# One TensorE, eight heads of attention and two mixers: the whole order of work written anew

## The chip, the cores and the metric

The kernel runs on one core of a Trainium2 chip. The metric is the device time of one execution in microseconds. The kernel before takes 292.22 us, the median of three runs (292.13 to 292.43).

## The reference

A block-sparse attention (each query block sees its neighbours, the first and the last block and three drawn blocks) over 4 batches, 8 heads, 768 positions and 64 elements is followed by a residual mixer: one linear layer over the 768 tokens, then a two-layer perceptron over the 512 channels.

```python
scores = np.where(mask, scale * (q @ k.T), -1e9)
attn = softmax(scores)
x = heads_side_by_side(attn @ v)                  # 4 x 768 x 512
a1 = alpha1 * x + beta1
u = x + lam * einsum('ts,bsd->btd', w_tok, a1)
a2 = alpha2 * u + beta2
out = u + lam * (maximum(a2 @ w_ch1, 0) @ w_ch2)  # 512 -> 2048 -> 512
```

## The kernel before

Two heads of one batch make a pair; there are 16 pairs, four to a batch. All of the work after a short preamble is written out as one long string, `ORDER`, of 1,589 words. A loop at the end of the kernel reads it word by word; the letters of a word pick a small function, the number says on which piece it works, and what follows a colon is a PSUM bank (for TensorE) or an engine (`d` VectorE, `a` ScalarE). Each engine, and each engine's DMA queue, then does its own words strictly in this order (`pin_order`); between engines an instruction waits for the data, the buffer or the bank that it needs (`bank_order` keeps one dependency per bank of the eight).

The words that the change and the prediction speak of:

- **lq, lk, lv** (line 437): load the queries, keys or values of a pair, with a cast to 16 bits, into one of six buffers (`NLD`). They are issued from GpSimd's queue, as are **lt** (two of the six slices of the token weights), **lc** (the small vectors: lam, alpha1 and beta1 spread over all partitions as lc0, lc1, lc2; be2T as lc4 and a2T as lc5), **lw** (line 479, one of four slices of the first channel weights, `w1b`) and **lx** (line 485, one of four slices of the second, `w2b`). A load of a pair from the eighth on waits for a flag that VectorE sets (**F**). The buffer of lx is that of the token weights, free when the last W is done.
- **cq, ck, cv**: copy the loaded pair to where it is used (line 421 on VectorE, 419 on ScalarE). This frees the load buffer.
- **H** (line 355): six transposes of a head's queries and keys into a bank; **hq, hk** copy them out. From pair 5 on a transposing DMA of SyncE's queue does this instead (**tq, tk**, line 593).
- **q** (lines 624 and 634): 1,024 columns of scores into two banks, banks 2j and 2j+1 for `:j`. Pairs 0 to 4 have nine such words each, in which the mask is 24 extra rows of the matmul; in the other pairs (line 634, 99 words) two 64-row matmuls run in two halves of the array and the mask is applied by VectorE (**m**). A word covers columns in order: q0 begins with the first key tile, q3 works on key tiles 4 and 5, and from q5 on (second half of a pair's nine) the pair's second head is used.
- **e** (line 645): the exponential of a q on ScalarE. **p, r** (line 661): its matmuls with the values. **n, nt**: the normalization.
- **a, b** (and halves ah, bh), **k** (line 763, 18 matmuls), **x**: the token mixer. **W** (line 496) and **w** turn the token weights; **L, S, T** fold lam and sums into weights; **U, u, v** turn the mixer's result into `uT`, with transposes on TensorE (U with a bank, line 806) or by DMA. **B** puts be2T beside it.
- **f** (line 828, four matmuls, one for each slice of w1b) and **g** (lines 842 and 844, behind a copy of a bias column for the first 16): the first channel layer with its maximum. **h** (line 907) and **o**: the second one. **Y, V, y, d, D**: the last two batches' first layer, in a scheme with fewer products.
- **M, N, O**: build the mask rows, write them to memory (line 538), read them back spread over the partitions (line 545). N and O stand in SyncE's queue with tq, tk, U by DMA and the stores **s**.
- **z**: a matmul of zeros of 480 columns, without use for the result. The preamble has more of them.

Before the words the preamble loads the first pair's queries and keys by separate queues, builds the mask, turns the first head, and copies it out in pieces:

```python
nc.vector.tensor_copy(out=kx[0][0:D, 0:P], in_=flatA[D:P, 0:P])      # line 393
nc.scalar.copy(out=qx[0][0:D, HS:S], in_=flatB[0:D, HS:S])
nc.vector.tensor_copy(out=qx[0][0:D, 0:HS], in_=flatA[0:D, 0:HS])
nc.vector.tensor_copy(out=kx[0][0:D, P:HS], in_=flatA[D:P, P:HS])
nc.vector.tensor_copy(out=kx[0][0:D, HS:S], in_=flatB[D:P, HS:S])    # line 397
```

Of the kernel before, what the change touches and what calls it, by code (L numbers as in the profile page):

```python
# [66 lines left out]
g10:a T1 f28:5 g26:a f20:4 g31:a T2 g25:a f16:1 ck8:a f7:2 a4 g4:a f23:6 g17:a T3 O0 f13:3 g7:a tq7  # L67
g28:a f18:0 cq8:d cv5:d g13:a f22:5 cv7:d tq6 g16:d g6:a f21:2 g23:d g22:a f27:1 g18:a tk8 P3:d
g20:a g21:d f14:3 g27:a P2:d f29:2 tk7 g14:a F34 b4 lk11 f30:0 g29:d lk9 tq8 cq11:d q53:2 g30:a
q48:1 P4:d k9:1 e53 lk12 A8 A0 lv8 e48 q50:3 q46:2 x9 h0:0 lq10 e46 A9 A1 h14:1 e50 A4 q52:1 o0  # L70
q49:2 e52 q45:3 A2 h1 A10 e49 h2 o12 A11 e45 h15 m48 P0:a F27 m50 lq9 q51:1 q47:2 m49 p48:6 e47 k8:7
F43 m45 m46 e51 p49 p50 o1 q58:2 x8 q56:1 e58 nt16 h16 m51 e56 m52 q60:2 q59:3 h3 o13 e60 A3 p45:2
m58 e59 p46 h17 m53 u8:a m47 u9:a q57:2 q55:3 F36 o2 e57 p47 U4 o14 p51:3 m59 h4 ck11:a m56 p52 e55
p53 nt15 lk14 q63:2 nt17 h18 e63 o3 q64:1 m57 q54:3 e64 q71:2 m60 h5 o15 e54 p57:2 a5 p58 h6 e71 b5
p59 ck12:a m64 q70:2 q62:3 nt19 e70 h19 lk10 m71 e62 q69:1 m54 q61:2 h20 F47 A5 ck9:a m55 p54:6
cq9:a k11:7 lv11 o16 e61 o4 tq9 lq13 h7:1 x11 cq10:a m62 k10:0 tk9 e69 m61 lv9 p60:7 A6 q67:2 tq10
m69 p55 e67 p56 o6 q80:1 x10 p61 e80 p62 nt18 q66:2 h8 nt20 e66 m70 q78:1 ck10:a q68:3 a6 p69:0 e68
p70 lk13 h9 m66 b6 e78 p71 o7 q65:2 q76:3 m63 u10:a q75:1 e65 nt23 h10 m67 u11:a p63:0 cv8:d k12:4
e76 m65 U5 lq12 m68 p66:5 e75 p64 x12 p67 tk10 p68 o8 q81:3 nt22 q86:1 e81 p65 h11 nt21 e86 m75
q74:2 q73:3 a7 e74 k13:0 b7 e73 q72:1 x13 q77:2 o9 u12:a k14:0 u13:a m76 e72 U6 k15:6 x14 A7 e77  # L80
p75:0 p76 x15 q79:1 u14:a m72 q85:2 u15:a h12 m77 e79 U7 m73 p77 e85 q82:3 m80 q93:1 s5 h13 m78 e93
tq11 m79 p78:4 p72:5 m74 e82 p73 p79 tk11 o10 p80 p74 q84:1 P1:d q87:3 nt24 e84 s0 f37:1 m86 tk12
f35:5 e87 nt26 f39:2 ck13:d g35:a m84 lq14 f54:3 g37:a nt25 g39:a q89:2 cv9:d q95:3 e89 q94:0 g54:d
lv10 f38:2 m82 e95 f32:3 P5:d P7:d f34:4 g32:a P6:d f48:5 e94 ck14:d m85 lk15 p84:3 a8 g34:a q83:3
q98:0 e83 p85 cq12:d f47:4 F44 F41 cv11:d tq12 lv15 m81 e98 p86 f61:6 g47:d lv12 g48:a p81:7 m83
q92:0 g61:a q88:2 b8 g38:a p82 f49:6 nt28 e92 m98 f36:2 e88 g49:d f63:3 m89 g36:a q106:0 m87 q91:2
g63:a p83 f51:6 e106 nt27 f56:2 m88 g51:a p87:3 cq13:d e91 f41:7 V0 m94 p88 g56:a q90:0 q96:2 cv10:d
g41:a m93 f52:2 e90 m92 p89 f57:6 m95 g52:a f53:7 e96 V2 p93:2 nt29 g57:a q97:0 q99:2 cq14:d e97
f33:3 m96 tq14 m91 p94 e99 p95 k16:6 m97 tk13 g33:a nt31 g53:a q104:0 m90 q102:1 s2 e104 q103:2 x16
f62:7 s1 a9 e102 tq13 p90:6 p91 p96:0 m99 p92 g62:a p97 nt30 tk14 p98 e103 f60:1 nt32 q113:1 m104  # L90
g60:a q100:2 s3 q105:3 e113 m102 s4 f59:0 b9 k17:1 e100 m113 F45 m103 lq15 e105 f55:2 x17 f44:3 lv14
g59:a m100 g55:a q108:2 m106 q107:0 lv13 e108 q101:3 m105 k18:2 a10 e107 p102:4 f50:5 m108 e101 x18
p99:0 p100 b10 g50:a f58:1 m101 g44:a p103 g58:a q131:3 m107 q115:1 p105:5 A20 e115 f45:1 A12 p106
e131 p104 A16 p101 p107 nt33 g45:a q112:1 k21:6 nt34 e112 nt35 q116:0 A21 q111:1 e116 q130:2 a11
# [5 lines left out]
p129:6 u19:a p130 m128 p131 e117 U9 k23:7 a12 e132 h40 o26 U10 nt43 cv15:a h41 x23 b12 u23:a q138:1  # L100
m127 q118:2 q119:3 e118 o34 h32 V5 cv13:a h21:0 m132 e119 m134 k25:4 o27 e138 k24:5 A14 x25 q142:1
o18 q143:3 A15 p126:4 p127 e143 x24 h33 m118 e142 p132:5 m117 h34 m138 p133 o28 p134 q141:1 nt44
q139:3 e141 p117:1 m143 p128 p118 h22 e139 nt42 m119 q135:1 a14 q125:2 e135 k22:6 b14 u24:a p119
# [975 lines left out]
```

## Time and profile before

| | |
|---|---|
| median of the runs, lowest, highest | 292.22, 292.13, 292.43 us |
| the profiled execution | 291.82 us |
| its span, first to last instruction | 290.1 us |
| granted TensorE clock | 1.0 throughout |
| busy: TensorE matmuls, weight loads | 283.9 us (98%), 213.6 us (74%) |
| busy: VectorE, ScalarE, GpSimd | 263.8 us (91%), 234.0 us (81%), 53.3 us (18%) |
| read from HBM, written | 31.16 MB, 6.88 MB |

The busy time of TensorE is modelled to the end of each matmul and so contains short waits. The chain of waits goes back from the last instruction to what released it, step by step; its pieces in order of time carry the start, the length, the engine and the line. For a load the view by tile gives the issue time and the time to landing. In the rows of stretches of time each engine's busy time stands with its count of instructions, then the clock, the DMA share (the sum over the packets in flight, so over 1 is possible) and GB/s.

### The profile page before, as it was taken

Reading aid. Unit: us, or ns where it says so; the run is one execution under the profiler, and the core shown is the slowest. Engines: PE = TensorE matmul, PEld = TensorE weight load, DVE = VectorE, ACT = ScalarE, POOL = GpSimd, SP = SyncE. Lnnn points to the kernel's source line nnn. Section 1 sums busy time; section 2 is a strip of 40 time slices with the busy share of each in tenths; the row PEclk is TensorE's granted clock in tenths of the full one; section 3 lists DMA queues with packets and bytes.
Section 4 is the critical chain, followed back from the end, with each engine's and each line's share of the span. In section 5 each row is a group of like instructions: output and inputs, shape, how many; then the busy total and the mean of one; then the engine's idle time right before and its main releaser. Section 6 shows DMA issues by size and latency. Waiting matters only on the chain.

```text
span 290.1 us, 8529 instructions
## 1 busy us (share of the span) xinstructions
PE 283.9 (98%) x3538; PEld 213.6 (74%) x3538; DVE 263.8 (91%) x595; ACT 234.0 (81%) x350; POOL 53.3 (18%) x102
## 2 busy tenths in 40 slices
PE   8899999999999999999999999999999999999995
PEld 3677888755677878866677877888766788866884
DVE  5689997689999999999999999999999998699983
ACT  5999998849999999999999999968989860279500
POOL 8545734300621241024005000000000000000000
PEclk9999999999999999999999999999999999999999
DMA  6999999999983498499278002404110140330014
GB/s 161 189 246 210 195 211 194 203 165 176 168 115 30 53 140 118 74 164 135 27 186 146 7 2 57 85 3 47 37 75 0 19 112 0 148 145 1 2 42 177
DMA packets 47927, 30.95 MB, mean 107 GB/s; under 512 B 28792, under 2 KB 43984, under 8 KB 47888
## 3 DMA queue, kind: packets, MB, share of 16 engines
q0 software_dynamic: 15936, 15.21, 34.6%
q1 hardware_dynamic: 31340, 14.32, 24.3%
q10 hardware_dynamic: 612, 0.87, 0.8%
q8 instruction: 28, 0.46, 0.6%
q14 instruction: 11, 0.09, 0.1%
HBM read 31.16 MB, written 6.88 MB: 131 GB/s over the span
## 4 chain that ended last, share of the span: by engine, by line
PE 87%; ACT 5%; DMA 4%; DVE 2%; issue 1%; POOL 0%; ACTq 0%
PE psum L907 26%; PE psum L997 13%; PE psum L828 12%; PE psum L661 11%; PE psum L763 11%; PE psum L634 9%; PE psum L624 4%; DMA wtk<-in_moe_w_tok_dram 3%; ACT hts L842 2%; ACT eT L645 2%; DMA k2f<-in_k_dram 1%; PE psum L806 1%; PE psum L355 1%; DVE a1p L733 0%; ACT rel L419 0%
## 5 line engine op out<-in xcount | busy, mean ns | idle before, releaser
L645 ACT ACTIVATE eT<-psum 128x1024 f16<-128x1024 f32 (+1 forms) x145 | 140.4, 1028 | 9.3 <-PE psum L634 5.4
L655 DVE TENSOR_TENSOR eT<-eT,maskT 128x960 f16<-128x960 f16 x99 | 61.2, 650 | 0.0
L907 PEld LDWEIGHTS <-hts 128*128 128x128 bf16 x480 | 45.1, 98 | 8.5 <-issue 2.1
L661 PEld LDWEIGHTS <-eT 128*128 128x128 f16 x1152 | 44.4, 97 | 8.3 <-issue 1.7
L661 PE MATMUL psum<-vext,eT 128*128 128x65 f16 x1152 | 48.5, 193 | 0.0
L828 PE MATMUL psum<-uT,w1b 128*128 128x384 bf16 (+1 forms) x256 | 45.9, 327 | 0.1
L1023 ACT ACTIVATE snap<-psum,b1t 128x384 f32<-128x384 f32 x44 | 23.7, 581 | 17.7 <-PE psum L997 13.4
L763 PE MATMUL psum<-a1p,wtokT 128*128 128x128 bf16 x576 | 36.8, 219 | 0.2 <-DVE x_sb L772 0.2
L763 PEld LDWEIGHTS <-wtokT 128*128 128x128 bf16 x576 | 33.2, 98 | 4.1 <-DVE x_sb L772 0.8
L907 PE MATMUL psum<-w2t,hts 128*128 128x256 bf16 x288 | 35.8, 273 | 0.0
L866 DVE TENSOR_TENSOR x_sb<-x_sb,psum 128x256 f32<-128x256 f32 (+1 forms) x61 | 30.7, 514 | 4.7 <-PE psum L907 4.5
L828 PEld LDWEIGHTS <-w1b 128*128 128x128 bf16 x256 | 23.0, 98 | 16.1 <-ACT b1t L419 0.9
L842 ACT ACTIVATE hts<-psum,b1t 128x384 bf16<-128x384 f32 x53 | 29.2, 602 | 0.9 <-PE psum L828 0.5
L634 PE MATMUL psum<-qx,kx 64*128 64x256 bf16 x396 | 29.8, 272 | 0.0
L866 DVE TENSOR_TENSOR hts<-snap,psum 128x384 bf16<-128x384 f32 x48 | 24.7, 547 | 2.7 <-PE psum L997 2.3
L624 PE MATMUL psum<-qx,kx 88*128 88x512 bf16 (+1 forms) x120 | 25.8, 326 | 1.3 <-ACT eT L645 1.0
L907 PE MATMUL psum<-w2b,ss 128*128 128x256 bf16 x192 | 24.6, 273 | 0.0
L907 PE MATMUL psum<-w2b,hts 128*128 128x256 bf16 x192 | 24.4, 273 | 0.0
L634 PEld LDWEIGHTS <-kx 64*128 64x128 bf16 x396 | 15.2, 94 | 8.4 <-issue 3.5
L907 PEld LDWEIGHTS <-ss 128*128 128x128 bf16 x192 | 18.0, 98 | 3.8 <-issue 0.6
L772 DVE TENSOR_TENSOR x_sb<-x_sb,psum 128x384 f32<-128x384 f32 x32 | 17.4, 546 | 1.0 <-PE psum L763 0.8
L997 PEld LDWEIGHTS <-w1b 128*128 128x128 bf16 x128 | 12.1, 98 | 6.6 <-DVE hts L866 0.3
(103 smaller groups left out, 362.5 us busy)
## 6 DMA issues: line engine op xcount, KB each, us to landing
out_dram<-x_sb SPq DMA_DIRECT2D x17, 256.0 KB, 2.6
v<-in_v_dram POOLq DMA_DIRECT2D x16, 192.0 KB, 6.3
k<-in_k_dram POOLq DMA_DIRECT2D x15, 192.0 KB, 6.2
q<-in_q_dram POOLq DMA_DIRECT2D x15, 192.0 KB, 7.1
w2b<-in_moe_w_ch_dram POOLq DMA_DIRECT2D x4, 512.0 KB, 12.0
w1b<-in_moe_w_ch_dram POOLq DMA_DIRECT2D x4, 512.0 KB, 12.9
wtk<-in_moe_w_tok_dram POOLq DMA_DIRECT2D x3, 384.0 KB, 8.3
out_dram<-x_sb SPq DMA_DIRECT2D x2, 512.0 KB
```

The lines of the kernel that those rows point to most:

```text
L624: nc.tensor.matmul(t[:, f : f + w], kx[h][0:KC, ts(jt, P)], qx[h][0:KC, c : c + w], start=True, stop=True,)
L634: nc.tensor.matmul(t[:, (2 * a + j) * TH : (2 * a + j + 1) * TH], kx[h][r, ts(2 * g + j, P)], qx[h][r, ts(th, TH)], start=True, stop=True,)
L645: nc.scalar.activation(eTs[n][:, c], t[:, c], AF.Exp, bias=EXPB, scale=SCALE)
L655: nc.vector.tensor_tensor(out=e, in0=e, in1=mask, op=ALU.min)
L661: nc.tensor.matmul(ops[key][:, t * VW : t * VW + D + 1], eTs[n][:, c : c + P], vext[n // NU % NV][:, a, jt, 0 : D + 1], start=(first and z ...
L763: nc.tensor.matmul(t[:, j, :], wtokT[:, s, ts(3 * g + j, P)], a1p[p][:, s, :], start=(s == 0), stop=(s == NT - 1),)
L828: nc.tensor.matmul(hps[i][:, 0:w], w1b[:, dk, ts(f, P)], uT[b][:, dk, hf * HS : hf * HS + w], start=(dk == 0), stop=(dk == 3),)
L842: nc.scalar.activation(hts[kk][:, f, :], t[:, 0:HS], AF.Relu, bias=b1t[:, f : f + 1], scale=1.0)
L866: nc.vector.tensor_tensor(out=out, in0=in0, in1=in1, op=op)
L907: nc.tensor.matmul(cps[b, q][:, side * HD : (side + 1) * HD], lhs[:, nk, :], rhs[:, nk, :], start=(z in (0, 6) and nk == 0), stop=(nk == H ...
L997: nc.tensor.matmul(chains[key], lhs[:, dk, ts(f, P)], rhs[:, dk, :], start=(z in (0, 1, 5) and dk == 0), stop=(dk == 1), skip_group_check= ...
L1023: nc.scalar.activation(dst, t, act, bias=bias, scale=1.0)
```

## The change

Nothing but the string `ORDER` is changed: the same 1,589 words (by kind and number) in another order, with other banks and in places another engine behind the colon. The order of GpSimd's loads is different: it began lv0 lk1 lq1 lt1 lq2 lk2 lv1 lq3 lt0 lt2 lk3 lc2 lc0 lc1 and begins lv0 lq1 lk1 lq2 lt1 lk2 lv1 lt0 lt2 lc1 lc2 lc0 lk3 lv2 lq3; the small broadcast vectors now stand ahead of the keys and queries of pair 3, the fourth pair of heads. The diff, cut after the first lines of each side (through the first f and g words):

```diff
 ORDER = """
-lv0 lk1 lq1 q0:0 lt1 q3:1 cq0 e0 lq2 q2:2 H1:6 lk2 e2 hq1:d q1:0 lv1 z480:7 hm0 z480:7 e1 hk1:d
-cv0:d q5:2 ck1:d e3 lq3 q4:0 p0:6 lt0 e4 p1 p2 lt2 q6:1 cq1:d e5 p3 lk3 p4 H2:7 H3:0 lc2 e6 hk2:d
-q7:2 lc0 F35 W2:1 hq2:d e7 lc1 q8:1 hq3:d r4:7 lk4 r5 w2:d e8 q9:2 cq2:d r6 F24 ck2:d lv2 r7 e9 n0
-z480:1 q12:1 lq6 hk3:d r8 e12 q11:2 n1 W3:6 q10:0 e11 w3:d H5:7 cv1:d q16:1 hk5:d e10 lq4 H4:6 hk4:d
-W1:4 e16 q15:0 hq5:d p9:5 e15 p10 hq4:d q13:1 F21 cq3:d W0:7 F46 w1:d e13 lv4 q14:0 p11 W5:4 e14
-ck3:d q25:1 F22 w0:d lk5 p12 w5:d e25 p13 q19:3 n2 W4:4 e19 H6:0 F28 lx3 w4:d q22:1 hk6:d r13:1
-q17:2 e22 L1 q20:3 hq6:d e17 q24:1 L0 r14 H7:0 e20 q18:2 ck4:d a0 lv3 r15 e18 r16 r17 lc5 b0 q23:3
-e24 cv2:d k1:4 n3 lk6 e23 lx1 q21:1 cq4:d r22:1 F42 x1 H9:5 e21 lv6 q28:3 F38 a1 p18:4 lw0 e28 r23
-F40 q26:1 b1 p19 e26 hk9:d p20 r24 p21 hq7:d r25 cq6:a q27:3 cv4:d hq9:d r26 lq7 e27 p22 q30:1 hk7:d
-k0:5 lw3 n5 e30 lc4 L2 H8:0 F23 F32 x0 q35:3 lw1 hk8:a hq8:d q31:1 lw2 k3:5 n4 e35 lx2 cv3:d q29:0
-ck5:a x3 lq5 q32:3 ck6:d e31 k2:4 lk7 a2 e29 lx0 b2 p27:5 q34:1 x2 lv7 p28 u0:d e34 p29 p30 u3:d p31
-lq8 r31:4 q33:0 e32 F37 n6 k4:2 e33 q39:3 x4 r32 u2:a F29 r33 e39 r34 r35 q37:0 n7 q38:1 U1:5 F25
-ah6 e38 q40:3 ah7 k5:4 cv6:d e37 bh7 lk8 bh6 q36:1 cq7:d e40 x5 k7:0 lv5 F33 u4:d e36 B0 k6:1 x7
-u1:a M0 p36:0 v1:a F39 u5:d p37 p38 x6 q41:1 u6:d U0:1 e41 q43:2 u7:d U2:6 S6 p39 e43 U3:7 v0:d
-q44:1 v2:a v3:d p40 q42:2 F26 S7 r40:1 r41 e44 f0:6 f6:7 e42 f3:2 g0:a f5:3 cq5:d g3:d f1:6 tq5 lq11
-g5:a F31 n8 r42 f8:2 N0 r43 g8:d f17:0 tk5 f24:3 r44 g24:d f9:2 tk6 S1 f11:3 g9:a g1:d f15:4 ck7:a
-S4 f25:2 g11:a n9 f19:5 F30 S3 f12:1 S2 f2:3 g12:a S0 f31:6 g19:a S5 g15:a f26:1 T0 g2:a f10:4 f4:3
...
+lv0 lq1 lk1 lq2 lt1 q3:0 q2:1 lk2 cq0 e3 q0:2 hm0 lv1 H1:6 e0 z480:7 hq1:d q1:0 lt0 z480:7 F41 F21
+hk1:d lt2 z480:7 e2 cv0:d lc1 q8:2 e1 q5:3 lc2 p0:2 lc0 e5 q4:0 lk3 p1 ck1:d e4 cq1:d q6:3 lv2 p2
+cq2:d H2:3 e6 lq3 F24 H3:0 hk2:d r4:1 p3 lq4 e8 p4 hq2:d q7:3 lw3 r5 n0 r6 e7 q10:2 lc5 hq3:d q9:1
+e10 lw1 ck2:d r7 hk3:d H4:6 lv3 r8 e9 hq4:d q13:2 W3:0 hk4:d e13 q11:1 w3:d q15:3 n1 e11 W2:0 H5:4
+w2:d W1:5 e15 q14:1 cv1:d hq5:d lk4 q12:0 e14 w1:d W0:6 W5:7 hk5:d W4:5 e12 F28 w0:d q16:1 p9:4
+w5:d e16 p10 q17:0 w4:d q23:3 L0 e17 q25:1 L1 r13:5 p11 e25 p12 ck3:d q22:0 a0 lv5 p13 e23 r14 r15
+lx0 n2 r16 r17 e22 q24:1 F37 b0 lc4 q18:3 F23 cv2:d e24 k0:4 n3 lq8 e18 q20:0 x0 r22:5 q19:1 cq3:d
+e20 a1 q26:3 lv4 H6:4 e26 r23 lw2 hk6:d q21:0 r24 b1 e19 r25 r26 hq6:d p18:6 H7:7 e21 n5 q28:1 p19
+F40 hq7:d e28 q30:2 F26 hk7:d p20 p21 e30 p22 cq4:d q27:0 F42 n4 lq5 q31:1 e27 k3:7 cv3:d lx2 F22
+e31 lx3 q32:0 x3 q33:2 e32 L2 lw0 q29:1 a2 lq7 p27:6 p28 e33 q35:0 b2 k2:7 ck4:d e29 F38 u0:d lv6
+H8:4 e35 B0 H9:5 x2 p29 hq9:d p30 hk8:a p31 r31:7 q34:0 hq8:d k5:2 u2:a hk9:d e34 n6 r32 q40:2
+cv5:a x5 k1:6 u5:d e40 lq6 F30 ah6 r33 q39:0 u3:a cv4:d F27 x1 lk7 r34 e39 r35 M0 q43:1 cq5:d
+q36:2 bh6 u1:a lv7 tq5 n7 q38:0 e43 k4:6 lx1 F29 ah7 N0 e36 bh7 q41:1 F46 x4 k7:7 e38 u4:d F47 S5
+e41 k6:6 S4 q42:0 F39 x6 U2:2 e42 x7 q37:2 cq8:d p36:3 u6:d r40:6 lk5 e37 U1:7 u7:d U0:0 r41 v0:d
+v2:a U3:1 p37 v3:d p38 v1:a r42 q44:2 S6 p39 e44 f1:2 r43 g1:a p40 f7:7 cv6:a r44 f11:2 n9 lk6
+f17:0 ck7:a n8 f18:1 cq6:a a4 f13:3 cv7:a F25 cq7:d f2:6 lk8 S7 g7:a f3:4 g11:d lq9 g13:a f27:5
+lk9 f12:7 g27:a f9:2 S2 f10:3 g17:d f15:5 g3:d f23:0 F32 F34 F36 g9:d f4:4 g23:a S3 f19:2 g2:a S0
+f29:0 g18:a g15:d f25:6 g10:a S1 f8:1 g19:a T0 g12:a f5:5 g4:a f14:7 ck5:d g25:a T1 tk5 f26:4 g8:a
+f0:6 g5:a T2 ck8:a f21:1 f16:5 g21:a ck6:d T3 tk6 f31:2 g0:a f28:1 g31:a b4 O0 f6:6 g14:a g26:d
...
 """
```

More of the change, by code (lines that the diff above doesn't have):

```diff
@@ L67 @@
[L67 to L94, printed above, removed]
@@ L100 @@
[L100 to L103, printed above, removed]
-e125 x22 h23 m141 u22:a q120:1 nt39 q140:2 e120 q137:3 U11 m142 k29:1 o19 e140 V1 k28:2 m125 u25:a
-x29 e137 p141:3 U12 p142 m120 p143 h24 u29:a m139 m140 q123:2 q121:3 o20 e123 p138:1 x28 p139 h25
@@ new lines @@
+q62:1 q71:3 m68 e62 p56 lq13 h18 nt18 e71 m61 q65:1 k10:0 o4 e65 m67 q69:3 cq12:a F35 o15 q66:1
+k11:4 e69 m63 s5 lv11 o6 tq10 h19 e66 x11 m65 q64:3 cq11:a tk10 q70:1 x10 p60:4 m62 u8:a p61 lk13
+h8 e70 m69 tq11 m66 p62 e64 h20 A6 U4 cv9:a nt20 q78:1 q73:3 m70 p66:0 u10:a lk12 h9 e73 o16 m64
+p63:4 p67 e78 p69:5 o7 p68 m71 q72:3 u11:a q75:1 a6 e72 p70 U5 h10 m78 e75 p64 b6 p65 q79:3 nt22
+cq13:a q80:1 p71 nt21 e80 k12:0 lq14 nt23 e79 o8 q86:1 x12 q84:2 h11 a7 e86 A7 q85:3 e84 q76:1 b7
+k13:0 e85 m79 k15:4 m80 P0:a x13 k14:5 o9 u12:a x15 e76 p78:0 x14 p79 q74:3 u13:a m72 h12 e74 m73
@@ new lines @@
+k16:0 tq12 cv10:a m95 e90 f33:1 nt27 lv12 cq14:d q94:2 x16 g33:a q92:3 q96:1 m90 e92 f34:0 tq14 a9
+f57:1 e94 f62:6 tk13 g57:d g34:a f50:7 m94 e96 p93:0 m92 s1 f39:1 g62:a tq13 m97 p94 g50:a p95 b9
+g39:a q107:1 m96 q103:2 s2 e107 q102:3 nt31 k19:1 m106 e103 p90:0 x19 p91 e102 p96:2 cv11:d p92
+ck14:d p97 nt30 p98 tk14 u16:a q113:2 nt32 q99:3 e113 f59:3 a10 q101:0 g59:a q100:2 m107 f58:2
+e101 m113 f37:3 e100 b10 f63:0 m101 e99 k18:1 F44 V4 lv14 m100 g58:a lv13 q105:2 g37:a m99 q116:3
+f56:2 g63:a V0 lv15 p99:3 m102 g56:a k20:0 e105 x18 m103 f32:2 e116 A20 p102:1 p103 p100 x20 g32:a
@@ new lines @@
+y123 D116:a y148:2 nt45 D130:a y142 d122:a p120:7 m123 p121 d147:a y132 d125 y154:6 d141:a d151
+y149 D123:a y141:0 D125:d V7 d148:a y161:1 y143 d144 y145:2 d142:a p122 d132 y150 d154:a d145
+p123:0 y144 d161:a a15 y156 d149:a y155:3 p124 d143:a nt40 y163 d155:a y151 d158 p125 D132:a b15
+y162:5 d162:a y146 nt41 y166:3 D138:a y152:7 d146 D139:a y164 a13 d150:a y157 y159:0 D144:a k30:2
+d152 d156:a b13 d163:a d165 y153 D151:a k26:4 d166 D146:a D158:a d153 D165:a y167 d159 k27:5
+D137:a x26 D153:d u26:a D166:d y160 D145:a x27 h42:7 d160 u27:a d167 D117:a h56:4 U13 D159:a
```

76 lines of the change are left out of this document (46 added, 30 removed).

## The prediction

> **What bounds the kernel now.** I read the page, then the chain of waits, then the instructions in order of time for the first microseconds, then single loads by tile.
>
> ```profile
> by line: PE psum L907 25.6%; PE psum L997 12.6%; PE psum L828 12.3%; PE psum L661 11.5%; PE psum L763 11.1%; PE psum L634 8.8%; PE psum L624 4.2%; DMA wtk<-in_moe_w_tok_dram 2.8%; ACT hts L842 2.0%; ACT eT L645 1.8%; DMA k2f<-in_k_dram 0.9%
> ```
>
> Seven lines of TensorE alone carry 86% of the chain. Its pieces (start, length, what) give the price of each kind of TensorE's work and the places where something else led.
>
> ```profile
> 5.83 1.61 PE psum L624 x9
> ...
> 10.70 8.27 DMA wtk<-in_moe_w_tok_dram
> ...
> 21.99 0.92 ACT eT L645
> ...
> 26.80 0.34 PE psum L355 x6
> 27.13 0.44 PE psum L624 x3
> 27.57 0.73 PE psum L661 x24
> 28.30 0.44 PE psum L624 x3
> 28.74 1.16 PE psum L763 x18
> ...
> 53.94 3.27 PE psum L828 x20
> ...
> 84.48 1.00 PE psum L763 x18
> ```
>
> The prices: a score word (q) of the first five pairs 0.44; one value matmul (p, r) 0.73/24 = 0.030; six transposes (H, W, U) 0.34; a token-mixing word (k) 1.00; a hidden-layer word (f, four matmuls) 3.27/5 = 0.65. An exponential of 1,024 columns holds ScalarE for 0.92.
>
> From 5.83, where the first score starts, to 53.94, where the hidden layer starts, lie 48.1 us. The words ahead of the first f (f0 in the order before) hold 45 q (19.8), 336 value matmuls (10.1), 8 k (8.0), 19 groups of six transposes (6.5) and three fillers of about 0.2 (0.6, 480 columns against 512 in the 0.22 piece that I take from the 0.44 of a q): 45.0. So TensorE waited about 3.1 us there. By 28.74 the same count (25 q, 144 value matmuls, 13 groups, the fillers: 20.4) leaves 28.74 - 5.83 - 20.4 = 2.5 of them. This is nearly all that another order can win, because the matmuls themselves are the same in both orders. One of the early waits is a load's: the chain stands on the token weights until 10.70 + 8.27 = 18.97, when W1 may start.
>
> **The change part by part.** The 1,589 words are the same; their order, the banks and some engines change. On ScalarE stand cv 9 times instead of 4, ck 3 instead of 8, cq 7 instead of 3, D 31 instead of 28, d 57 instead of 60, g and u one fewer each: two more in sum, at most 2 x 0.72 (a cast, below). I cost this at nothing, since TensorE's work hides it; if ScalarE led there it would be 1.4. Four of the casts get a price of their own below, for where they stand.
>
> *The start.* The first score is now q3 instead of q0. In order of time, from the kernel before:
>
> ```profile
> 6.39 0.11 PEld L624 LDWEIGHTS <-kx 88*128 88x128 bf16 x2 [0.18 <-DVE kx L397]
> ```
>
> q3 reads key tiles 4 and 5, which the copy of line 397 writes last; its weights waited for that copy until 6.39 there too, behind q0. So TensorE starts 0.56 later, and the first exponential comes at 6.39 + 0.44 + 0.1 = 6.95.
>
> *The first scores.* From there ScalarE sets the pace through the banks: a q may start when the exponential that emptied its bank has ended. The tightest such place in the new order, by counting, is q35, which follows the exponential e32: 32 exponentials end at 6.95 + 32 x 0.92 + 0.1 = 36.5. The TensorE work ahead of q35 (34 q, 232 value matmuls, 2 k, 13 groups, fillers) is 28.9, so 5.83 + 28.9 = 34.7, and 1.8 us of waits are forced, the late start included. The old order had 2.5 by 28.74. W1 is not held up any more: q3's load of pair 3 (lq3) now stands behind lt0 and lt2, so lt0 lands a head's load (1.0, below) earlier, at about 18.0, and W1 is due at about 18.9. Between 28.74 and 53.94 the old order gained another 0.6 of waits; with that TensorE would be ready for its first f (f1) at 5.83 + 45.1 (340 value matmuls) + 1.8 to 2.4 = 52.7 to 53.3, that is 0.6 to 1.2 before 53.94.
>
> *The loads ahead of f1.* Every f reads all four slices of w1b (lw0 to lw3). Loads by tile, with issue time and time to landing:
>
> ```profile
> L479 POOL DMA_DIRECT2D w1b<-in_moe_w_ch_dram x2: 571/576/581, 36.0 to 36.5; - x2
> DMA to landing us min/median/max: 14.3/14.9/15.6
> L485 POOL DMA_DIRECT2D w2b<-in_moe_w_ch_dram x1: 755/755/755, 38.5 to 38.5; - x1
> DMA to landing us min/median/max: 16.1/16.1/16.1
> L437 POOL DMA_DIRECT2D q<-in_q_dram x1: 706/706/706, 39.7 to 39.7; - x1
> DMA to landing us min/median/max: 15.9/15.9/15.9
> L485 POOL DMA_DIRECT2D w2b<-in_moe_w_ch_dram x1: 765/765/765, 44.4 to 44.4; - x1
> DMA to landing us min/median/max: 14.8/14.8/14.8
> L437 POOL DMA_DIRECT2D q<-in_q_dram x1: 713/713/713, 56.3 to 56.3; - x1
> DMA to landing us min/median/max: 11.1/11.1/11.1
> ```
>
> The last w1b slice (lw2) landed at 36.5 + 15.6 = 52.1, 1.8 before it was needed; lx2 at 54.6; lq5 at 55.6; lx0 at 59.2; lq11 at 67.4. Issue to landing is 11 to 16 us: the loads stand in one queue that never empties, so landings are a sum. A head's load costs 55.6 - 54.6 = 1.0; lk7 and lx0 together 3.6, so an lx 2.6. In the new order the last slice is lw0. Ahead of it and with it stand 16 head loads, all three lt, five lc, four lw and three lx; in the old order lx2 has the same with 18 head loads. So lw0 lands at 54.6 - 2 x 1.0 = 52.6, if nothing else uses the DMA engines.
>
> Something does. tq5 and N0, the first transposing DMA and the write of the mask rows, are issued right behind the cast of pair 5's queries (cq5) in both orders:
>
> ```profile
> 56.10 1.32 SPq L593 DMA_TRANSPOSE qx<-rel  x1
> 57.47 0.83 SPq L538 DMA_DIRECT2D mask_rows<-maskT  x1
> ```
>
> ```profile
> 45.00:56.00 11.00, 11.00 (x158) 8.59 (x156) 8.88 (x26) 10.18 (x13) 3.68 (x9) 1.00 1.18 203
> 56.00:60.00 4.00, 4.00 (x46) 2.68 (x44) 2.42 (x9) 0.81 (x3) 0.71 (x1) 1.00 1.40 188
> 60.00:64.00 4.00, 4.00 (x26) 2.18 (x24) 3.93 (x10) 2.21 (x6) 0.00 (x0) 1.00 1.39 119
> ```
>
> The last column is GB/s: 203 with the loads alone, then 188 and 119 when the others had joined. After lq5 the old kernel still got lk7 and lx0 in 3.6, without loss, and the next five head loads (to lq11) in 8.2 instead of 5.0: 3.2 lost. There that cost nothing, since f0 had started. In the new order lq5 stands ahead of lx2, lx3 and lw0, so tq5 and N0 go out at about 45 (52.6 less three large loads) and compete with them. lw0 comes 7.8 of load time after lq5; by the rows the loss is between 0 and (7.8 - 3.6)/5.0 x 3.2 = 2.7. It is nearer to the late rows, but there tk5 and tk6 were in the queue too, which now stand behind most of the f words; I take half, 1.3. Then lw0 lands at 53.9 and f1 starts at 54.0: **+0.1**, between -1.2 and +1.5.
>
> *Casts in ScalarE's queue.* Behind g1 the new order has cv6, ck7, cq6 and cv7 on ScalarE, and g7 behind them. Pieces of the chain of before:
>
> ```profile
> 66.92 2.00 ACT hts L842 x4
> 68.91 0.72 ACT rel L419
> ```
>
> A cast is 0.72, a g of this stage 0.50 and, with its small copy, about 0.65 (an estimate). With lw0's landing as zero, f1 starts at 0.1 and g1 ends at 1.5. The loads behind lw0 are lq7, lv6, lq6, lk7, lv7, landing at 1, 2, 3, 4, 5: cv6 ends at 2.7, ck7 waits for 4.0 and ends at 4.7, cq6 5.4, cv7 6.2, g7 6.8. f12 needs g7's bank and is reached after nine f and 20 value matmuls, 6.5 behind f1's start: 6.6. A wait of 0.2. With heads at 8.2/5 = 1.64 each it is 3.0 (lk7 6.6, lv7 8.2, g7 9.6). I take 0.5, nearer the first, since the tk transfers are not there.
>
> *Switches of the array.* From the sixth pair on the scores (line 634) use half of the rows each.
>
> ```profile
> 93.00 0.32 PE psum L634 x4
> 93.32 0.98 PE psum L907 x8
> 94.30 0.76 PE psum L634 x12
> 95.06 0.98 PE psum L907 x8
> 96.04 0.49 PE psum L661 x16
> 96.53 0.87 PE psum L907 x8
> ```
>
> An h word is 0.87, but 0.98 behind a run of such scores: 0.11. Eight more score matmuls make 0.32 into 0.76, so four are 0.22 and the other 0.10 of the 0.32 is the switch into the run. A run costs 0.2 beside its work. The old order groups the 99 score words in 46 runs, the new one in 49: 3 x 0.2 = **+0.6**. It lies on TensorE, which has no gap to hide it in; bounds 0 and 0.6.
>
> *What stays.* The work ahead of the first score and the last dozen words are the same. Pair 3's later keys and queries cost nothing: behind lt0 (18.0) lq3 has lt2 (twice a head's bytes, by its shape: 2.0), three small broadcast loads (at most 1.3 each, 4/3 of a head's bytes) and lk3, lv2 ahead of it, so it lands by 18.0 + 2.0 + 4.0 + 3.0 = 27.0. H6, which needs it, has 21.1 of TensorE work ahead: 5.83 + 21.1 + 1.8 = 28.7. If that cover of 1.7 were gone, each us more would be one lost.
>
> The sum: 0.1 + 0.5 + 0.6 = +1.2, on the profiled execution's 291.82, whose span is 1.7 less (both are in the table above), gives 293.0. The median of the runs shown is 292.22, 0.4 over that execution, and so the forecast is **293.4 us**.
>
> **The rivals.**
>
> (a) *The loads keep up.* No loss to tq5 and N0: lw0 at 52.6, f1 at about 53.0 (-0.9), f12's wait 0.2, switches +0.6: -0.1, 292.1. For it: 3.6 of load after lq5 went without loss. Against: 119 GB/s in the row that follows.
>
> (b) *Faster.* As (a), but early waits stay at 1.8, f1 starts at 52.7 (-1.2), and ScalarE, being half empty after the casts, no longer leads in the hidden layer, as it does in the chain before from 66.92 to 68.91 + 0.72 (I put 0.4 on such places, an estimate: half a g's length at two of them). -1.2 + 0.6 - 0.4 = -1.0: 291.2. It decides by lw0: landing before 52.7 it is possible, later not.
>
> (c) *The queues share evenly.* The loss is the full 2.7 (f1 at 55.4, +1.5), f12's wait about 1.5, switches 0.6: +3.6, 295.8. For it: by their shapes N0 writes three heads' loads of bytes and tq5 moves one, four against the 7.8 of load time that they meet. [...] The trace agrees from 60 on (119 GB/s, late heads) and not from 56 to 60.
>
> **How the numbers follow.** The forecast has 0.42, (a) 0.22, (b) 0.20, (c) 0.16. What the measurement tells from no change is 0.2%, 0.6 us: faster means under 291.6, slower over 292.8. (b) and an edge of (a) are faster: 0.24. (a)'s rest and a little of the forecast's lower flank are the same: 0.22. The rest is slower: 0.54. The likeliest case's own range is 292.6 to 294.4; the range over the cases, leaving out half of (b)'s and (c)'s outer ends, is 291.2 to 295.7.
>
> **What would show it.** Start: the first L624 matmul at 6.4. Loads: the landing of the last w1b load against the first L828 matmul; 53.9 and 54.0 by the forecast, and a gap on TensorE released by w1b. Contention: GB/s dropping under 150 between 46 and 54. Casts: ScalarE waiting for k and q loads between 55 and 60, and L828 waiting for hts behind them. Switches: 49 runs of L634, with 0.98 beside 0.87 for L907. I am wrong if f1 starts before 53.2, or if another place after 60 us, such as VectorE falling behind on the lx loads, costs over 0.5.

## The result, and the profile after

| | before | after |
|---|---|---|
| median of the runs, lowest, highest | 292.22, 291.66, 296.34 us (22) | 292.94, 291.98, 295.24 us (22) |
| ratio, 95% interval | | 1.0031, 1.0015 to 1.0046 |
| the profiled execution, its span | 291.82, 290.1 us | 292.21, 290.5 us |
| single times over 293.5 | 2 of 22 | 6 of 22 |

The change costs 0.7 us by the medians (292.94 - 292.22) and 0.4 by the two profiled executions. The ratio compares the means (293.17 and 292.28) and leaves out one slow execution of before, 296.34, which is also one of its two times over 293.5. Line numbers of the kernel after are two higher than those of before.

The chain that ended last, by line, from the page of after:

```profile
PE psum L909 26%; PE psum L830 13%; PE psum L999 13%; PE psum L663 11%; PE psum L765 10%; PE psum L636 9%; DMA v<-in_v_dram 5%; PE psum L626 5%; ACT eT L647 2%; PE psum L317 1%; PE psum L357 1%; PE psum L498 1%; DVE qx L423 0%; ACT vext L421 0%; DVE hts L846 0%
```

The token weights (2.8% before) are gone from the chain. In their place stands a load of values (lv7), from 44.75 on. The pieces of the chain of waits of after show what hangs on it (start, length, what):

```profile
6.36 0.62 PE psum L626 x3
7.01 4.76 ACT eT L647 x6
...
44.75 13.91 DMA v<-in_v_dram
...
58.74 0.83 ACT vext L421
59.58 0.07 ACT b1t L421
...
59.67 0.58 ACT hts L844
60.25 0.06 ACT b1t L421
60.30 5.71 PE psum L830 x34
```

The first score stands at 6.36 and the first exponential at 7.01. lv7 lands at 58.66; cv7 (vext) runs until 59.58, g7 (b1t, hts) until 60.25, and only then f12 starts, at 60.30. ScalarE's instructions in order of time, with the idle time ahead of each in brackets, show the queue in front of g7:

```profile
57.00 0.83 ACT L421 COPY rel<-k 128x768 bf16<-128x768 bf16 x1 [1.69 <-DMA k<-in_k_dram]
57.74 0.83 ACT L421 COPY rel<-q 128x768 bf16<-128x768 bf16 x1
58.74 0.83 ACT L421 COPY vext<-v 128x768 f16<-128x768 f16 x1 [0.18 <-DMA v<-in_v_dram]
59.48 0.15 ACT L421 COPY b1t<-psum 128x1 f32<-128x1 f32 x1
59.67 0.58 ACT L844 ACTIVATE hts<-psum,b1t 128x384 bf16<-128x384 f32 x1
```

For 1.69 us ScalarE stood idle with g7's bank full behind ck7, cq6 and cv7. The view of one line, the hidden layer's matmuls between 50 and 72, gives their first start and the idle time of TensorE. Before:

```profile
L828 PE MATMUL psum<-uT,w1b x105: 324/327/338, 53.8 to 72.0; 128*128 128x385 bf16 x60, 128*128 128x384 bf16 x45
```

After:

```profile
L830 PE MATMUL psum<-uT,w1b x108: 325/327/337, 52.9 to 71.9; 128*128 128x385 bf16 x60, 128*128 128x384 bf16 x48
its engine sat idle before it (us, times) until:
  ACT b1t L421: 0.8, 1
```

The layer starts 0.9 earlier (52.9 against 53.8) and then waits once, 0.8 by the modelled end of the matmul ahead, 0.9 by the starts. (The prediction's 53.94 is where a piece of the chain begins; the first matmul of the line stands at 53.8.) The last pieces of the chain, before and then after, close the account:

```profile
284.00 2.96 PE psum L907 x27
```

```profile
283.93 3.40 PE psum L909 x31
```

The last matmul ends at 286.96 before and 287.33 after: +0.4. So 0.9 was won up to the hidden layer and 1.3 lost behind its first word.

The loads. Issue and time to landing of the last w1b load (lw0):

```profile
L481 POOL DMA_DIRECT2D w1b<-in_moe_w_ch_dram x1: 541/541/541, 37.6 to 37.6; - x1
DMA to landing us min/median/max: 12.7/12.7/12.7
```

It lands at 50.4 (37.6 + 12.7 before rounding), 2.5 before it is needed. The next two views show when tq5 and N0 were issued (44.53 and 45.90), and the traffic by queue (packets, MB, share) in the three stretches 44.5 to 48.4, 48.4 to 53.3 and 53.3 to 58.0. q0 is the queue of GpSimd's loads, q1 that of SyncE, with tq5 and N0:

```profile
44.53 1.32 SPq L595 DMA_TRANSPOSE qx<-rel  x1
45.90 0.83 SPq L540 DMA_DIRECT2D mask_rows<-maskT  x1
```

```profile
q0 software_dynamic: 515, 0.82, 115.6%
...
q0 software_dynamic: 827, 0.66, 89.4%
q1 hardware_dynamic: 806, 0.22, 38.7%
...
q0 software_dynamic: 745, 0.60, 80.2%
q1 hardware_dynamic: 385, 0.56, 39.3%
```

The loads move 0.82 / 3.9 = 0.21 MB per us alone, 0.66 / 4.9 = 0.13 beside tq5 and 0.60 / 4.7 = 0.13 beside N0. No packet of q1 moves from the issue of tq5 until 48.41, 3.9 us later. Then the loads lose more than a third of their pace (0.13 against 0.21) for ten microseconds, and most of that falls behind lw0's landing.

### The profile page after: what moved, and what is told of

Same layout as the page of the kernel before. It is cut to its first block, busy times and chain, and to the rows that moved or that the text cites. A ratio compares the mean times of both kernels' runs of the same rounds, so it can differ in the third digit from the quotient of the medians.

```text
span 290.5 us, 8525 instructions
## 1 busy us (share of the span) xinstructions
PE 284.6 (98%) x3538; PEld 213.9 (74%) x3538; DVE 265.4 (91%) x595; ACT 234.1 (81%) x350; POOL 53.0 (18%) x102
## 4 chain that ended last, share of the span: by engine, by line
PE 89%; DMA 5%; DVE 2%; ACT 2%; issue 1%; DVEq 0%; ACTq 0%
PE psum L909 26%; PE psum L830 13%; PE psum L999 13%; PE psum L663 11%; PE psum L765 10%; PE psum L636 9%; DMA v<-in_v_dram 5%; PE psum L626 5%; ACT eT L647 2%; PE psum L317 1%; PE psum L357 1%; PE psum L498 1%; DVE qx L423 0%; ACT vext L421 0%; DVE hts L846 0%
## 5 line engine op out<-in xcount | busy, mean ns | idle before, releaser
L647 ACT ACTIVATE eT<-psum 128x1024 f16<-128x1024 f32 x145 | 138.8, 1042 | 8.4 <-PE psum L636 6.0
L830 PE MATMUL psum<-uT,w1b 128*128 128x384 bf16 (+1 forms) x256 | 44.7, 327 | 0.8 <-ACT b1t L421 0.8
L1025 ACT ACTIVATE snap<-psum,b1t 128x384 f32<-128x384 f32 x41 | 22.1, 588 | 18.1 <-PE psum L999 16.3
L830 PEld LDWEIGHTS <-w1b 128*128 128x128 bf16 x256 | 23.8, 98 | 17.2 <-ACT b1t L421 1.2
L909 PE MATMUL psum<-w2t,hts 128*128 128x256 bf16 x288 | 34.9, 273 | 0.0
L844 ACT ACTIVATE hts<-psum,b1t 128x384 bf16<-128x384 f32 x52 | 28.0, 591 | 3.7 <-PE psum L830 3.2
L636 PE MATMUL psum<-qx,kx 64*128 64x256 bf16 x396 | 30.5, 272 | 0.0
L626 PE MATMUL psum<-qx,kx 88*128 88x512 bf16 (+1 forms) x120 | 24.7, 326 | 1.1 <-DVE kx L399 0.6
L636 PEld LDWEIGHTS <-kx 64*128 64x128 bf16 x396 | 14.5, 94 | 9.7 <-issue 3.6
L909 PEld LDWEIGHTS <-ss 128*128 128x128 bf16 x192 | 18.1, 98 | 3.9 <-DVE x_sb L868 0.4
L439 POOL DMA_DIRECT2D k<-in_k_dram x15 | 10.7, 714 | 33.5 <-DVE rel L423 19.6
```

The lines of the kernel that those rows point to most:

```text
L626: nc.tensor.matmul(t[:, f : f + w], kx[h][0:KC, ts(jt, P)], qx[h][0:KC, c : c + w], start=True, stop=True,)
L636: nc.tensor.matmul(t[:, (2 * a + j) * TH : (2 * a + j + 1) * TH], kx[h][r, ts(2 * g + j, P)], qx[h][r, ts(th, TH)], start=True, stop=True,)
L647: nc.scalar.activation(eTs[n][:, c], t[:, c], AF.Exp, bias=EXPB, scale=SCALE)
L830: nc.tensor.matmul(hps[i][:, 0:w], w1b[:, dk, ts(f, P)], uT[b][:, dk, hf * HS : hf * HS + w], start=(dk == 0), stop=(dk == 3),)
L844: nc.scalar.activation(hts[kk][:, f, :], t[:, 0:HS], AF.Relu, bias=b1t[:, f : f + 1], scale=1.0)
L909: nc.tensor.matmul(cps[b, q][:, side * HD : (side + 1) * HD], lhs[:, nk, :], rhs[:, nk, :], start=(z in (0, 6) and nk == 0), stop=(nk == H ...
```

## The experiments

Each is a move of words in `ORDER` (two also add fillers). Times are medians of the given number of runs; each ratio is to runs of the kernel before on the same chip. The kernel after was timed in the result's runs alone (ratio 1.0031), so a distance to it in microseconds reaches across chips. The theory was at first: the loss is f12's wait behind the casts (0.9) and three more runs of half-array scores (0.6), less the earlier start.

**g7 ahead of ck7** (in the kernel after).

```diff
-f17:0 ck7:a n8 f18:1
+f17:0 g7:a ck7:a n8 f18:1
...
-lk8 S7 g7:a f3:4
+lk8 S7 f3:4
```

> The changed order with one word moved: g7 now stands on ScalarE ahead of ck7, cq6 and cv7 instead of behind them. Theory (f12 waits for g7, which waits behind three casts whose loads come late): the 0.94 us wait ahead of f12 falls to under 0.2, the span falls by about 0.8 to 0.9, the time to about 292.1 (ratio to before 1.000). Rival (the +0.7 comes from the array's switches and from elsewhere, and what is won at f12 is lost again a few f words later because ScalarE is still blocked by the loads): a new wait at f10 or f15 of the same size, time 292.7 to 293.0.

292.98 us (12 runs), ratio 1.0021 (1.0000 to 1.0043). f12's wait is gone, and another has come behind it. The chain of waits of this kernel:

```profile
45.59 15.62 DMA w2b<-in_moe_w_ch_dram
...
61.23 0.04 DVE w2b L513
...
61.84 0.62 DVE hts L844
...
62.51 12.60 PE psum L828 x75
```

VectorE's S2 stood in its queue until lx1 landed at 61.2, and g17 behind it, so f23 came 0.5 late. The cast was a cause of the wait, as the theory has it; most of the gain went on to the next late load, as the rival has it.

**tq5 and N0 later in the text.**

```diff
-lv7 tq5 n7
+lv7 n7
...
-ah7 N0 e36
+ah7 e36
...
-T1 tk5 f26:4
+T1 tq5 N0 tk5 f26:4
```

> The changed order with tq5 and N0 moved down SyncE's order to directly ahead of tk5 (from about 44.5 to 68 us). Theory (these two compete with the loads behind lw0): lq7, lv6, lq6, lk7 and lv7 land 1.0 apart instead of 1.3 to 2.2, lv7 at 55.4 to 56 instead of 58.66, the wait ahead of f12 falls to 0.2 or less, and the time to about 292.0 to 292.3, with less scatter. Rival (the loads are slow there for another reason, such as the waits of their own buffers or many outstanding loads): lv7 still lands after 58, f12 waits 0.9, time 292.9. Price that can show in either case: the masks read back later (O0 behind N0) and VectorE's first mask word m45 at about 82 us waits; up to +1.

292.92 us (12), ratio 1.0025 (1.0008 to 1.0042). The two words passed no other word of SyncE's, and only the order on each engine counts: they were issued at 44.7 and 46.1, near the 44.5 and 45.9 of the kernel after. The move changed nothing and decides nothing; it is a second measurement of the kernel after.

**Ten more runs of half-array scores** (in the kernel before: 56 runs instead of 46, the same matmuls).

```diff
-q57:2 q55:3 F36 o2 e57 p47 U4
+q57:2 F36 o2 e57 p47 q55:3 U4
...
```

> The kernel before with ten score words of pairs 6 to 15 moved behind the value word that follows them, so that ten runs of half-array scores are split in two: 56 runs instead of 46, same matmuls. Theory (a run costs 0.2 beside its work): +2.0 us, 294.2, ratio 1.007. Rival (the switches are hidden or the 0.1 beside h and p is only how the ends of matmuls are modelled): within 0.2% of before, 292.2.

294.39 us (6), ratio 1.0073 (1.0051 to 1.0094): +2.1 us for ten runs, 0.2 each, with whatever waits the moves bring. In its profile the hidden layer starts late, at 54.9, but from there to the last matmul's end it takes 235.5 instead of 233.2, 2.3 more. The price of the prediction holds, on a TensorE with hardly a gap (3.6 us of idle time ahead of its matmuls in this profile's span of 293.6).

**q0 first again** (in the kernel after).

```diff
-lt1 q3:0 q2:1 lk2 cq0 e3 q0:2 hm0 lv1 H1:6 e0
+lt1 q0:2 q3:0 q2:1 lk2 cq0 e0 e3 hm0 lv1 H1:6
```

> The changed order with q0 moved ahead of q3 and e0 ahead of e3, as in the old order. Theory (TensorE and ScalarE start 0.5 earlier, but the time is set later by lv7's landing and g7): first score at 5.83 instead of 6.36, f1 0.3 to 0.5 earlier at 52.4 to 52.6, f12 still at 60.2 to 60.3, so no change, 292.9. Rival (the start is worth its 0.5 to the end, because nothing later takes it): 292.4.

292.44 us (12), ratio 1.0012 (0.9991 to 1.0033). The median is the one that the rival names, but the interval reaches over that of the kernel after, so the times decide nothing. In the profile the first score stands at 6.21, only 0.15 earlier, and the first exponential at 6.63, 0.4 earlier; the hidden layer starts at 53.1, not earlier than the 52.9 of the kernel after, and f12 waits 0.6 in the view of its line. The profile speaks for the theory; the next kernel is the better test.

**The late start alone** (in the kernel before: q3 ahead of q0).

```diff
-q0:0 lt1 q3:1 cq0
+q3:1 q0:0 lt1 cq0
```

> The kernel before, with q3 ahead of q0: the late start of the change, alone. Theory of the prediction (the first score waits for the copy of line 397 until 6.4 and all exponentials follow): the first exponential, e0, comes 0.5 to 1.0 later than 6.5, and because exponentials pace the first 29 us there, 0.4 to 1.0 of it reaches the hidden layer: f0 at 54.2 to 54.8, ratio 1.001 to 1.004. Rival (the early waits shrink by as much, as they did when the kernel after got q0 back in front): f0 at 53.7 to 54.0, ratio 1.000.

292.19 us (12), ratio 1.0004 (0.9986 to 1.0022). ScalarE's instructions, in the kernel before and in this one:

```profile
6.24 6.16 ACT L645 ACTIVATE eT<-psum 128x512 f16<-128x512 f32 x7 [0.46 <-PE psum L624]
```

```profile
7.24 5.67 ACT L645 ACTIVATE eT<-psum 128x512 f16<-128x512 f32 x7 [1.31 <-PE psum L624]
```

The first exponential is a full microsecond late, yet the first seven instructions end at 12.40 and at 12.91, half a microsecond apart, and the hidden layer starts at 53.9 instead of 53.8. The rival was right: the waits that follow shrink by nearly as much.

**lt0 first** (in the kernel before: lq3 moved behind lt0 and lt2, the change's small part alone).

```diff
-e3 lq3 q4:0 p0:6 lt0 e4 p1 p2 lt2 q6:1
+e3 q4:0 p0:6 lt0 e4 p1 p2 lt2 lq3 q6:1
```

> The kernel before, with lq3 (pair 3's queries) moved behind lt0 and lt2: the part of the change that puts small weights ahead of that head, alone. Theory: lt0 lands near 18.0 instead of 19.0, W1's wait of about 0.3 is gone, but TensorE is then paced by exponentials (2.5 us of waits by 28.7 in the kernel before), so half or more of it comes back in the waits that follow: 0.0 to 0.3 us under the kernel before. Rival (the whole early gain is this wait): 0.3 or more under it, and f0 starts at 53.5 or earlier instead of 53.8.

291.99 us (12), ratio 1.0000 (0.9986 to 1.0015). lt0 lands at 18.1, W1 no longer waits for it, and the hidden layer starts at 53.8 as before. Its chain goes over to the exponentials:

```profile
22.03 0.50 PE psum L496 x6
...
23.06 0.76 ACT eT L645
```

The first term of the chain that an eye falls on in the page of before, 2.8% on the token weights, was worth nothing.

**Three runs fewer** (in the kernel after: 46 instead of 49).

```diff
-m61 q65:1 k10:0 o4
+m61 k10:0 q65:1 o4
...
-m77 q82:3 p73 e82
+m77 p73 q82:3 e82
...
-o21 q137:2 x28 p141:2 e137
+o21 p141:2 q137:2 x28 e137
```

> The kernel after, with three words moved ahead of the run of half-array scores that they cut (k10 ahead of q65, p73 ahead of q82, p141 ahead of q137): 46 runs of scores instead of 49, as before. Theory (the loss of the change is its three runs more, 0.2 us each on TensorE, with nothing to hide them): 0.6 us under the kernel after, so a profiled span of about 289.9 and a ratio of about 1.001 to the kernel before; pure TensorE work 273.8. Rival (a run's switch hides in the waits for exponentials that follow, because the second score then starts earlier and waits for its bank): no gain, the gaps ahead of q69, q83 and q121 grow by 0.2 each.

294.37 us (6), ratio 1.0077 (1.0054 to 1.0099): worse by 1.4 than the kernel after, where the theory had 0.6 less. The chain of this kernel around the first place:

```profile
101.58 0.34 PE psum L634 x4
...
101.95 1.03 ACT eT L645
...
103.03 0.39 PE psum L634 x4
```

q66 uses the bank of q65, which now came 1.0 later; q66 waits 1.1 for the exponential between. That comes of where k10 was put. At the other two places the rival holds: q83 waits 0.14 and q89 0.25 more, y133 0.17, and the switches saved there are given back. These waits less three switches make about 1.0 (1.1 + 0.14 + 0.25 + 0.17 - 0.6). They are not the reason of the whole 1.4, though. In this profile the hidden layer starts at 54.4, 1.5 later than after, for a reason that lies ahead of the moved words (last section); and the kernel with grouping, g7 and S2 together, below, has the same three moves and the same wait of 1.1 at q66, and took 292.82. So a switch cost 0.2 where ten were added to a full TensorE (2.1, above), but these three could not be taken out for a gain of 0.2 each; what taking them out costs by itself stays open.

**The mask rows later** (in the kernel after: M0, for which N0 waits, and N0 around n8; N0 is issued at 56.7).

```diff
-r35 M0 q43:1 cq5:d
+r35 q43:1 cq5:d
...
-ah7 N0 e36
+ah7 e36
...
-ck7:a n8 f18:1
+ck7:a M0 n8 N0 f18:1
```

> The kernel after, with M0 (the compare that N0 waits for) and N0 moved to around n8, so that the write of the mask rows is issued near 56 instead of 46. Theory (N0 shares the queue's time with the loads from about 50 on): lw0 lands as in the kernel after, 50.4; the five loads behind it come 1.0 apart, lv7 near 55.5 to 56.5 instead of 58.7; the casts end earlier, f12 waits under 0.3 instead of 0.9; total 0 to 0.7 us less. Rival (the heads' loads are slow there for another reason, their own destinations coming free or their issue): lv7 stays within 0.5 of 58.7, f12 still waits 0.8 to 1.0, total unchanged. The other theory of the forecast (lw0 itself is held up) would have lw0 land earlier than 50.0.

292.24 us (12), ratio 1.0000 (0.9986 to 1.0015): 0.7 below the kernel after, the upper end of what was expected; the two intervals just meet, at 1.0015. In its profile all loads are a microsecond late from the start (lt0 lands at 19.0 instead of 18.0), so lengths have to be compared: from lw0's landing to lv7's it is 6.9 us instead of 8.3. f12 still waits, 0.5 in the view of its line, because lk7 landed at 57.8 only. That the mask rows cost the loads behind lw0 is borne out (1.4 us up to lv7), though not the 1.0 from head to head that the theory had. It is no accident of one profile: from lw0's landing to lv7's it is 8.0 to 8.9 us in the seven profiles of the new order with the rows early, and 5.8 to 7.3 in the three with the rows late (this one, and two below). The 0.7 of the medians is not explained by this profile, in which the last matmul ends 0.5 later than after.

**Grouping, g7 and S2 together** (in the kernel after: the three moves of the grouping, g7 ahead of ck7, S2 behind g9).

> The kernel after with the three words of the grouping moved, g7 ahead of ck7 on ScalarE, and S2 (the scaling that waits for lx1) behind g9 on VectorE: what the runs so far point to. Theory (the costs add up: 0.6 for three runs, 0.9 for f12's wait, and f23's new wait of 0.5 in the kernel with g7 moved alone was VectorE standing behind lx1): 1.3 to 1.5 us under the kernel after, span near 289.1, ratio 0.997 to 0.999 to the kernel before. Rival (the waits move on to the next g words whatever is moved, because TensorE is ahead of the hidden layer's copies): no wait at f12 and f23, but 0.5 or more in new ones before 75, and only the 0.6 of the runs is won.

292.82 us (12), ratio 1.0035 (1.0013 to 1.0057). f12 and f23 do not wait; f10 does, 0.6 in the view of its line, since g13 now stood behind cv7 and lv7 landed at 59.8; q66 waits 1.1 as above. The costs do not add up: that is the rival's case, without the 0.6 that it gave to the runs.

**Fillers ahead of q3** (in the kernel after).

```diff
-lt1 q3:0 q2:1
+lt1 z480:7 z480:7 z480:7 q3:0 q2:1
```

> The kernel after, with three filler matmuls of 480 columns (about 0.2 us each) ahead of q3, so that TensorE works through the 0.6 us in which it waits for the copy of line 399. Theory (the late first score has a second price: TensorE starts at half pace, 0.107 us from one 128-column matmul to the next, and comes to full pace at a moment that differs from execution to execution, 3.7 to 5.6 us in nine of the profiles and 10.3 in one, whose hidden layer began 1.5 late; the longer the idle stretch ahead of the first score, the more executions come to it late): full pace before 7.5 in the profile, f1 at 52.9 to 53.2, fewer executions above 293.5 (after had 6 in 22), median 292.4 to 292.8. Rival (the pace comes when it comes, or the scatter is all of the end's): the same share above 293.5, median 292.7 to 293.1.

292.62 us (12), ratio 1.0008 (0.9988 to 1.0028). Full pace came at 5.3 in the profile. Five of the twelve times are over 292.9 and one over 293.5 (6 of 22 after): too few to tell. f12 waited 1.1 there, with lv7 at 59.3.

**Rows later, and the late casts behind the g words that TensorE needs** (in the kernel after: M0 and N0 as above, ck7 and cq6 behind g13, cv7 behind g27, S2 behind g9).

```diff
-f17:0 ck7:a n8 f18:1 cq6:a a4 f13:3 cv7:a F25
+f17:0 M0 n8 N0 f18:1 a4 f13:3 F25
...
-g13:a f27:5 lk9 f12:7 g27:a f9:2 S2 f10:3
+g13:a ck7:a cq6:a f27:5 lk9 f12:7 g27:a cv7:a f9:2 f10:3
...
-F36 g9:d f4:4
+F36 g9:d S2 f4:4
```

> The kernel after, with M0 and N0 around n8, on ScalarE ck7 and cq6 behind g13 and cv7 behind g27, and S2 behind g9 on VectorE. Theory (the hidden layer's first waits come from copies that stand behind late loads, and the mask rows make the loads late): no wait over 0.3 at f12, f10 or f23, f1 at 52.9 when lt0 lands near 18; 0.9 under the kernel after in the profile, median 291.6 to 292.1, a ratio of 0.998 to 1.000 to the kernel before. Rival (TensorE is ahead of the copies of the hidden layer, so a wait of about 0.8 comes at another f word, as f10 in the kernel with g7 moved and the words grouped): 0.5 to 0.8 us at another f before 72, median 292.2 to 292.6.

292.25 us (12), ratio 0.9999 (0.9980 to 1.0018). ScalarE's instructions in this kernel:

```profile
55.31 0.16 ACT L419 COPY b1t<-psum 128x1 f32<-128x1 f32 x1
55.51 0.58 ACT L842 ACTIVATE hts<-psum,b1t 128x384 bf16<-128x384 f32 x1
58.02 0.16 ACT L419 COPY b1t<-psum 128x1 f32<-128x1 f32 x1 [1.93 <-PE psum L828]
58.21 0.58 ACT L842 ACTIVATE hts<-psum,b1t 128x384 bf16<-128x384 f32 x1
58.69 0.82 ACT L419 COPY rel<-k 128x768 bf16<-128x768 bf16 x1
```

g7 runs at 55.3, ScalarE waits for TensorE and not the other way round, and no f waits longer than 0.3 (f13). The last matmul ends at 286.8, 0.5 before the kernel after. So in the profile the waits that the casts made are gone, as the theory has it. The median is that of the kernel with the mask rows alone moved (292.24): what the moved casts add shows in the trace, not in the times. Four of the twelve times lie at 293.0 to 293.4, the others at 291.6 to 292.7.

**The same with the three fillers.**

> The kernel with M0, N0, the casts and S2 moved (the row e10), and with the three fillers ahead of q3. That kernel's twelve times stand in two groups, seven at 291.6 to 292.3 and four at 293.0 to 293.4. Theory (the upper group is a late full pace of TensorE at the start): the fillers empty it, at most one time in twelve above 292.9, median 291.6 to 292.0, which would beat the kernel before. Rival (the upper group is the end: packets of the last store that stand behind an instruction fetch for about 1.5 us, which the fillers do not touch): three to five of twelve above 292.9 again, median 292.0 to 292.6.

292.02 us (12; 291.58 to 292.25), ratio 0.9991 (0.9974 to 1.0008). No time is above 292.3, as the theory has it, though the run was on another chip than the kernel without the fillers. This version takes back what the change cost, but is not to be told from the kernel before.

## Why the prediction came out as it did

The time (292.94 against 293.4) lies in the likeliest case's own range and the sign is right. Of the three terms of the sum, the casts had the right mechanism and half the size, the switches the right price, and the start of the hidden layer was wrong, which by the prediction's own condition (f1 before 53.2) makes it wrong: f1 stood at 52.9. With the measured sizes the sum is -0.9 + 0.9 + 0.6 = +0.6 instead of +1.2, and the trace has +0.4. That the number still came within the range is in part luck: the load term missed by 1.0, and 0.4 of that came back at f12, because an f1 that starts earlier waits longer for the same g7.

*Start.* q3 at 6.36, first exponential at 7.01 against 6.95: right. (The prediction's own sum, 6.39 + 0.44 + 0.1, is 6.93.) That it need not cost anything was not said; the kernel with the late start alone shows it.

*Early waits, W1.* TensorE was to be ready for f1 at 52.7 to 53.3; it started at 52.9, with 52.9 - 5.83 - 45.1 = 2.0 us of waits (forecast 1.8 to 2.4). lt0 was to land at 18.0 and did. Alone, in the old order, the earlier lt0 moved nothing.

*The loads ahead of f1: +0.1 forecast, -0.9 measured.* This step failed, twice over. First, "the last slice is lw0 ... at 52.6, if nothing else uses the DMA engines": it landed at 50.4, with tq5 already moving for 2.0 us. The pace was not the reason. Up to 50.4 us q0 had moved the same 9.00 MB in both kernels, before and then after; the third line is the kernel before up to 54.6, when lx2 landed. (The new order was 0.16 MB ahead at 48.4, 8.75 against 8.59, and the time beside tq5 took that back.)

```profile
q0 software_dynamic: 7623, 9.00, 103.5%
...
q0 software_dynamic: 7537, 9.00, 102.3%
...
q0 software_dynamic: 8581, 9.85, 105.2%
```

By their shapes, lx2 and all loads ahead of it are 9.18 MB, so 0.67 MB of later loads had moved when it landed; lw0 and all ahead of it are 8.79 MB, and only 0.21 were over. The difference, 0.46 MB, is 2.2 us at 0.21 MB per us: the whole of 52.6 - 50.4. And it is no property of the old order: in the kernel with the late start alone, which has that order, q0 had moved 9.02 MB by 50.4, and lx2 landed at 52.5 (54.8 and 54.1 in the two other kernels that have the same loads ahead of it). So one landing stood up to 2.3 us off another with the same loads ahead of it (52.5 to 54.8), and the prediction hung its sum on one landing of one profile. Why a landing lags behind the bytes was not tried and stays open. Second, "tq5 and N0 go out at about 45 and compete": they were issued at 44.5 and 45.9, but their packets began at 48.4. The issue time was taken for the start of the traffic. The kernel before had misled in the same way: there tq5 was issued at 56.10, but no packet of q1 moved until 58.7, so the 3.6 us of loads that "went without loss", up to 59.2, lay nearly all ahead of the competition. The competition itself was larger than the 2.7 that the prediction held for the most: by the rows above 4.9 + 4.7 - (0.66 + 0.60) / 0.21 = 3.6 us of load time. Most of it fell on the heads behind lw0. The sign that the prediction had named for it, GB/s under 150, did not come (175 from 48 to 52 and 239 from 52 to 56), because that column counts both queues; only the rows by queue show the loss.

*Casts in ScalarE's queue: +0.5 forecast, 0.9 measured.* The mechanism is right, place by place: ck7 and cv7 wait for their loads, g7 stands behind them, f12 waits for g7. The upper bound went by heads at 1.64; from lw0 to lv7 there are five, in 58.7 - 50.4 = 8.3 us, 1.65 each. The wait was not the 3.0 of that bound, since lw0 came 3.5 earlier than in the sum (50.4 instead of 53.9) and f1 1.1 earlier (52.9 instead of 54.0): 3.0 - (3.5 - 1.1) = 0.6, and 0.9 came. The kernels with g7 moved and with all late casts moved show the cause: f12's wait is gone in both.

*Switches: +0.6.* Three runs more at 0.2. Ten more runs cost 2.1 on the chip, so the price is shown. That it is the whole reason why TensorE's work grew is worked out, not shown: behind the start of the hidden layer 1.3 were lost, 0.9 at f12, 0.6 by the runs, less 0.1 for four value matmuls that stand ahead of it in the new order and 0.1 in all other waits. Taking three runs out won nothing. The 0.6 is therefore a price times a count, not a measured part of the 1.3.

*Pair 3's loads.* The last of lq3 landed at 25.2 (27.0 at most by the prediction): no cost, right.

*The rivals.* (a) was right that the loads would not hold up f1 (53.0), though not on lw0's landing (52.6), and wrong on f12 (0.2). (b)'s earlier start of 52.7 came nearly true, and so did its second half behind f12: from 60.30 the chain of after has one piece of 15.17 us of the hidden layer alone, where that of before goes over to ScalarE again and again (66.92, 68.91). What (b) left out is f12's wait: 0.9, more than the 0.4 that it put on those places. (c) had the two queues share evenly. Counted in packets, the rows above agree with it beside tq5 (827 and 806), and less beside N0 (745 and 385). In bytes it is the other way round (0.66 and 0.22 MB beside tq5, 0.60 and 0.56 beside N0), because tq5's packets are small (0.22 MB in 806) and the loads' three times as large (0.66 MB in 827). How the DMA engines choose between two queues no run here shows. (c) was right on the size of the loss (3.6, it had 2.7), and wrong on its place, as the forecast was: its f1 at 55.4 came at 52.9.

By the trace the change costs 0.4, by the medians 0.7. The difference is in the scatter (6 of 22 times over 293.5 after), of which the last section shows two sources in single profiles. The runs give a third hint: of the new order with the mask rows early (after, g7 moved, tq5 and N0 later in the text, q0 first, fillers) 15 of 70 times lie over 293.5, and with the rows late none of 36, though the chips differ too. Which source weighs most in the kernel after is open.

## What to carry to other kernels

A DMA's traffic started well behind its issue (the first packet of tq5 moved 3.9 us behind it after, 44.53 to 48.41, and 2.6 before, 56.10 to 58.72): read the packets by queue in stretches of time before deciding which loads it will meet. A landing read from one profile is not a fixed point to add to: the same order of loads put lx2 at 52.5 and at 54.6. A wait that heads the chain was worth only the gap to the next wait behind it: removing the token weights' wait alone (ratio 1.0000 to the kernel before), or one blocked g word alone (292.98 against 292.94 us), won nothing. In an in-order queue, a copy that waits for a load belongs behind the copies that free banks; here that took the waits out of the trace (no f waited over 0.3 us, against 0.9), though not more out of the medians than moving the mask rows alone (292.25 against 292.24).
